# Sparse attention into a gated feed-forward layer: the softmax reciprocals of units 2 to 7 spread over the partitions by VectorE's shuffle instead of through DRAM, in a new order of all instructions

## The chip, the cores and the metric

One core of a Trainium2 chip runs the whole kernel in one launch. The metric is the device time of an execution in microseconds (us). Engines are TensorE (PE in the profile; PEld is its weight load), VectorE (DVE), ScalarE (ACT), GpSimd (POOL) and SyncE (SP). SP here only issues DMAs; four more are issued from ScalarE's queue at the start.

## The reference

Batch 4, 8 heads, 768 positions, head width 64. Heads 0, 2 and 6 ("retrieval") attend to all earlier positions, the other five only to the first 4 positions ("sinks") and to a window of 64. Then the heads are laid side by side and a two-matrix layer follows.

```python
scores = scale * np.matmul(q, k.transpose(0, 1, 3, 2))      # 4 x 8 x 768 x 768
stream_keep = causal & (is_sink | in_win)                     # sink: pos < 4, window: 0 <= rel < 64
mask = np.where(retrieval head, causal, stream_keep)
a = np.exp(scores - max); a = a / (sum(a) + 1e-9)             # where mask, else 0
x = np.matmul(a, v)  ->  (3072, 512)
h = x @ w_in                                                 # 512 x 2048
g = h * (1.0 / (1.0 + np.exp(-beta * h)))
out = g @ w_out                                              # 2048 x 512, float32
```

## The kernel before

**Units.** The work is cut into eight units: unit n is batch n // 2 and half u = n % 2 of the sequence, 384 positions. For each unit, `attention` loads q, k and v, casts them to bf16, brings q and k into head-width-major form (units 0 to 2 by TensorE transposes, units 3 to 7 by a transposing DMA, `turn_block`), computes scores transposed (`scores`, in "rounds" into one of two PSUM tiles `sp`), exponentials on ScalarE (`exps`, into tiles `es`), masks on VectorE (`masks`), sums over the keys by matmuls with selecting columns (`sums`, `sums_d`), and the product with v (`pv`). The result, normalized by the reciprocal of the sums, is `xT` (512 rows by 384 positions in bf16, four tiles of 128).

**The layer behind it.** `first` does one of 16 steps of the first product per unit: four matmuls of 128x384 (`mm1`), then `swish_a` (Tanh on ScalarE, tile `t`) and `swish_b` (VectorE, tile `gT`). A step needs a cast column block of w_in (`cast_w_in`, 16 pieces, four to a load) and all of `xT`. `second` does the product with w_out three matmuls at a time, `out_copy` and `out_store` end it.

**The reciprocals.** Units 0 and 1 (`recips`, `split`, `spread`, `norm_held`) spread the reciprocal over the partitions with matmuls. Units 2 to 7 did it like this: `sums_d` leaves eight rows of 384 sums in PSUM, `sums_copy` brings them to an SBUF tile `sc`, `sums_turn` turns them by DMA into a tile `rec` of 96x32, `recips_d` takes the reciprocal there, `spread_w` stores it to DRAM (`rd`), and `spread_r` reads it back so that each of the eight rows lies on 64 partitions of `R` (128 x 4 x 384 f32). On odd units one more part goes to a tile `RX`, since the last third of one head's product is computed on the other half of the partitions (`moved`). `norm` multiplies PSUM by `R` into `xT`. `R` is one buffer, so the next unit's spread waits for this unit's `norm`.

**The order.** Nothing is left to a scheduler. Every operation is added to a plan with what it needs, what it gives and which buffers it takes; `SEQUENCE` lists all operations in the order in which the plan takes them, and `CHOICE` says for some of them which of two or three engines runs them. The plan places each operation by costs written in `add`, and the instructions are issued in order of that placing. So each engine's queue is fixed in advance: an instruction that waits holds all that stand behind it on its engine. A matmul `fill` before some steps of units 0 and 1 repeats transposes of a constant for gaps that the plan foresees, and 25 such matmuls open the program. Rings say how many buffers a name has: `wf` (weights and later q, k, v blocks, 1 MB or 0.8 MB each) 3, `vf` 3, `q2f` and `k2f` 5, `b` (PSUM bank) 4, `sp` 2, `osb` 3, `R`, `rec` and `sc` 1.

All instructions are issued through one helper, so every line of the profile says L112, and groups are told apart by tile names.

Of the kernel before, what the change touches and what calls it, by code (L numbers as in the profile page):

```python
# [8 lines left out]
F32 = mybir.dt.float32  # L9
# [11 lines left out]
NQ = 384  # L21
# [7 lines left out]
QUARTERS = [[[1, 0], [2, 3], [4, 5], [6, 7]], [[2], [6], [0], [3, 5, 7, 1, 4]]]  # L29
ROWS = [16, 1]  # L30

NE = [16, 24]
ORDER = [[1, 0, 2, 3, 4, 5, 6, 7], [2, 6, 0, 3, 5, 7, 1, 4]]
# [4 lines left out]
    474, 475, 6, 466, 4, 8, 14, 468, 12, 478, 467, 20, 10, 0, 2, 16, 5, 469, 473, 9, 7, 33, 471, 29, 77, 34,  # L38
    31, 13, 89, 32, 15, 30, 37, 477, 18, 50, 38, 39, 51, 11, 79, 40, 85, 1, 56, 43, 52, 3, 490, 35, 25, 41,
    27, 36, 26, 57, 42, 28, 17, 44, 45, 21, 47, 78, 91, 48, 53, 80, 97, 54, 59, 86, 102, 480, 23, 100, 24,  # L40
    101, 58, 103, 60, 49, 116, 19, 46, 117, 118, 55, 61, 22, 120, 62, 463, 121, 485, 479, 492, 119, 122, 73,
    493, 90, 63, 92, 491, 123, 114, 75, 64, 74, 81, 115, 112, 76, 83, 125, 481, 65, 87, 126, 67, 113, 69, 484,
    66, 134, 482, 71, 68, 135, 483, 137, 108, 70, 500, 139, 109, 72, 488, 520, 82, 93, 524, 138, 84, 104, 464,
    140, 127, 489, 95, 465, 528, 521, 494, 105, 522, 529, 486, 532, 536, 495, 136, 525, 487, 530, 106, 142,
    526, 88, 533, 143, 534, 502, 540, 107, 98, 110, 503, 547, 505, 111, 94, 541, 128, 548, 131, 501, 542, 551,
    132, 124, 555, 141, 129, 96, 549, 556, 559, 133, 159, 130, 560, 504, 557, 99, 144, 552, 510, 499, 553,
    155, 145, 497, 537, 498, 538, 157, 156, 496, 146, 515, 507, 563, 158, 509, 561, 570, 508, 564, 160, 147,
    523, 571, 148, 506, 527, 565, 572, 163, 531, 167, 153, 149, 151, 511, 535, 171, 150, 512, 161, 152, 574,
    513, 165, 154, 578, 575, 514, 173, 582, 579, 576, 169, 580, 586, 583, 218, 518, 592, 584, 476, 587, 517,
    596, 588, 516, 470, 597, 519, 539, 593, 598, 162, 543, 546, 594, 168, 222, 550, 172, 554, 174, 170, 184,  # L50
    185, 558, 544, 164, 166, 562, 190, 186, 188, 191, 193, 175, 189, 566, 187, 600, 221, 196, 569, 573, 192,
    601, 577, 194, 581, 567, 219, 181, 602, 198, 220, 604, 199, 197, 182, 224, 608, 201, 200, 585, 609, 195,
    227, 225, 203, 605, 610, 589, 223, 204, 606, 228, 612, 202, 206, 590, 205, 619, 613, 207, 226, 176, 208,
    620, 177, 623, 621, 209, 591, 614, 210, 627, 631, 229, 628, 635, 632, 629, 237, 633, 636, 235, 642, 568,
    624, 637, 239, 646, 238, 650, 211, 647, 625, 240, 212, 178, 472, 269, 595, 651, 648, 241, 599, 652, 242,
    654, 179, 643, 249, 655, 603, 236, 252, 644, 213, 658, 250, 253, 607, 656, 659, 244, 660, 611, 247, 271,
    615, 245, 618, 622, 243, 251, 616, 254, 248, 273, 626, 180, 255, 630, 257, 183, 634, 246, 256, 638, 258,
    272, 641, 639, 259, 270, 617, 645, 260, 649, 261, 214, 216, 231, 215, 280, 653, 232, 657, 217, 275, 661,
    664, 662, 274, 278, 668, 665, 276, 672, 669, 666, 277, 676, 262, 673, 230, 233, 670, 674, 677, 279, 678,
    680, 684, 681, 691, 682, 263, 685, 695, 326, 692, 686, 699, 693, 696, 703, 700, 697, 707, 663, 701, 714,  # L60
    704, 708, 718, 289, 705, 709, 715, 722, 726, 716, 264, 723, 234, 667, 727, 290, 281, 671, 724, 293, 282,
    728, 675, 719, 283, 291, 730, 720, 679, 731, 292, 315, 284, 295, 732, 683, 296, 687, 298, 690, 694, 688,
    300, 297, 698, 319, 303, 294, 327, 301, 302, 702, 304, 328, 706, 265, 299, 329, 267, 266, 689, 305, 330,
    545, 268, 710, 306, 713, 717, 307, 721, 370, 725, 317, 736, 729, 737, 321, 740, 738, 316, 711, 733, 324,
    741, 744, 318, 734, 748, 320, 742, 745, 752, 322, 749, 746, 323, 756, 308, 753, 750, 763, 754, 325, 757,
    767, 764, 758, 771, 640, 765, 768, 775, 309, 772, 366, 769, 779, 773, 776, 786, 777, 790, 787, 286, 780,
    788, 334, 332, 285, 739, 335, 287, 794, 336, 781, 743, 795, 310, 337, 791, 796, 747, 338, 792, 798, 339,
    369, 802, 799, 346, 367, 803, 800, 751, 349, 373, 368, 804, 755, 347, 376, 759, 762, 288, 760, 341, 372,
    766, 344, 333, 375, 770, 340, 342, 371, 774, 343, 374, 351, 350, 345, 778, 354, 348, 377, 782, 352, 785,
    311, 353, 355, 313, 312, 356, 789, 357, 314, 793, 358, 386, 797, 331, 387, 735, 801, 390, 712, 412, 808,  # L70
    388, 812, 809, 378, 392, 813, 810, 805, 395, 379, 814, 816, 391, 783, 359, 380, 820, 806, 817, 360, 824,
    416, 821, 818, 828, 822, 825, 835, 393, 826, 839, 396, 829, 836, 397, 830, 843, 389, 837, 840, 847, 361,
    844, 841, 851, 394, 848, 845, 415, 858, 849, 862, 852, 413, 859, 866, 853, 414, 860, 870, 863, 417, 864,
    400, 811, 419, 871, 815, 398, 418, 872, 422, 819, 867, 823, 868, 421, 399, 874, 401, 381, 827, 875, 420,
    402, 876, 362, 403, 404, 364, 363, 761, 831, 834, 423, 365, 838, 842, 429, 846, 880, 832, 850, 405, 881,
    431, 406, 882, 884, 807, 432, 382, 383, 888, 885, 892, 889, 886, 384, 854, 424, 890, 893, 857, 433, 861,
    426, 833, 855, 865, 407, 894, 869, 385, 896, 900, 425, 897, 434, 898, 907, 436, 911, 901, 784, 908, 873,
    902, 856, 877, 909, 912, 915, 878, 913, 919, 430, 916, 879, 427, 923, 920, 917, 930, 924, 921, 934, 435,
    925, 938, 931, 942, 932, 939, 408, 943, 940, 410, 409, 935, 883, 887, 411, 946, 944, 443, 936, 947, 891,
    895, 446, 447, 948, 952, 444, 953, 438, 954, 899, 441, 903, 439, 956, 442, 445, 906, 957, 448, 437, 958,  # L80
    910, 449, 914, 451, 450, 440, 918, 904, 960, 452, 453, 922, 454, 961, 926, 455, 964, 962, 968, 965, 905,
    929, 969, 933, 966, 937, 970, 428, 941, 945, 927, 949, 456, 972, 928, 950, 457, 979, 973, 983, 980, 974,
    987, 981, 984, 991, 988, 985, 995, 989, 992, 1002, 996, 993, 458, 1006, 997, 1003, 1010, 1007, 1004, 1014,
    1008, 1018, 1015, 955, 1011, 1016, 1012, 1019, 951, 1020, 959, 963, 967, 971, 975, 978, 976, 982, 977,
    986, 990, 994, 998, 1001, 999, 1005, 459, 460, 1000, 461, 1009, 462, 1013, 1017, 1021, 1024, 1022, 1028,
    1025, 1023, 1032, 1029, 1026, 1036, 1030, 1033, 1040, 1037, 1034, 1044, 1038, 1041, 1051, 1045, 1042,
    1055, 1046, 1052, 1059, 1056, 1053, 1063, 1057, 1060, 1067, 1064, 1061, 1073, 1065, 1068, 1076, 1069,
    1079, 1077, 1027, 1080, 1078, 1031, 1081, 1074, 1082, 1075, 1085, 1083, 1035, 1086, 1084, 1039, 1087,
    1043, 1047, 1048, 1050, 1054, 1049, 1058, 1062, 1066, 1070, 1088, 1071, 1089, 1072, 1092, 1090, 1091,
    1093, 1094, 1095,  # L90
]
CHOICE = (
    "aaddagaggdgdadadadaadddaddaaddgaagggdaaadaadaaaddaaaddaggdgdgaggadggdgdaadaadaaadaadadadddadddaaa"
# [95 lines left out]
def kernel(  # L189
# [68 lines left out]
    hl = consts.tile([96, NQ], BF16, name="hl")  # L258
# [49 lines left out]
    def const_zero():  # L308
        dve.memset(hl, 0.0)
        dve.memset(KP[2][:, 0:32 * (NP - 1)], 0.0)  # L310
# [185 lines left out]
    def load_beta():  # L496
        held["beta"] = rp.tile([128, NQ], F32, name="sc")[0:FO, 0:128]
        sp.dma_start(out=held["beta"], in_=moe_beta.rearrange("(fo fi) -> fo fi", fi=128))
# [278 lines left out]
    CR = NQ // 32  # L777

    def sums_turn(x):

        x.rec = rp.tile([8 * CR, 32], F32, name="rec")
        for p, step, c, n in ([(0, 16, 0, 8)], [(96, 1, 3, 5), (0, 32, 0, 3)])[x.u]:
            sp.dma_start(out=x.rec[c * CR:(c + n) * CR, :],
                         in_=x.sc[p:p + (n - 1) * step + 1:step, :].rearrange("p (c n) -> p c n", n=32))
# [4 lines left out]
    def spread_w(x):  # L789
        x.rd = dp.tile([8, NQ], F32, name="rd")  # L790
        sp.dma_start(out=x.rd.rearrange("h (c n) -> (h c) n", n=32), in_=x.rec)

    def spread_r(x):
        x.R = rp.tile([128, NP, NQ], F32, name="R", bufs=RINGS["R"])
        src = x.rd[:]
        at = [[ORDER[x.u].index(XT[t][i]) for t in range(NP)] for i in range(2)]
# [444 lines left out]
```

## Time and profile before

| | |
|---|---|
| median of 3 runs | 240.53 us (240.43 to 241.18) |
| span of the profiled execution | 238.9 us |
| its own time | not listed beside the span; the median is 1.6 us above the span |
| TensorE | 224.3 us busy (94%), mean granted clock 0.979 |
| VectorE | 153.9 us (64%) |
| ScalarE | 141.9 us (59%) |
| GpSimd | 90.8 us (38%) |
| DMA | 43.14 MB moved, 92108 packets, 75936 of them under 512 B |

A group's line has the engine, the operation, tile out <- tiles in, the shapes and the count; then the busy time in us and the mean ns of one; then the idle time of the engine just before, and what ended it. A timeline line has the start, the time from the first to the last of a merged group, the engine and operation. A window line has the stretch, its length, then each engine's busy time with its instructions, TensorE's granted clock (1.00 is full), the mean busy share of the 16 DMA engines and GB/s.

### The profile page before, as it was taken

How to read it: one execution, taken by the hardware profiler on the slowest of the kernel's cores; microseconds unless marked ns; L12 is line 12 of the kernel's file. 1: busy time of each engine (PE TensorE's matmuls, PEld its weight loads, DVE VectorE, ACT ScalarE, POOL GpSimd, SP SyncE). 2: the span in 40 equal slices, each digit the busy share in tenths (PEclk: the TensorE clock that was granted, in tenths of full speed). 3: DMA queues.
4: the chain of work that ended last, by engine and by line, in shares of the span. 5: the costliest groups of instructions: out<-in, count | busy, mean ns of one | idle time of the engine just before them, and what ended most of it. 6: DMA issues, size and time to landing. Idle time of an engine off the chain costs nothing.

```text
span 238.9 us, 6057 instructions
## 1 busy us (share of the span) xinstructions
PE 224.3 (94%) x2359; PEld 128.6 (54%) x2385; DVE 153.9 (64%) x354; ACT 141.9 (59%) x238; POOL 90.8 (38%) x199
## 2 busy tenths in 40 slices
PE   8678996999999999999999999999999999999994
PEld 8535555555555456546544545564465555466553
DVE  4539869783968838865686548787475477157620
ACT  3858785456889518761679569707677437107611
POOL 7204759587632845696536173403600000000000
PEclk9956999999999999999999999999999999999999
DMA  6999699999989979999998999789910026211012
GB/s 197 273 307 321 205 258 354 300 314 211 175 196 240 211 162 189 214 230 223 225 231 179 169 230 231 149 178 216 219 71 3 0 92 150 80 44 47 0 44 88
DMA packets 92108, 43.14 MB, mean 181 GB/s; under 512 B 75936, under 2 KB 84848, under 8 KB 92080
## 3 DMA queue, kind: packets, MB, share of 16 engines
q1 hardware_dynamic: 90992, 41.98, 76.0%
q10 hardware_dynamic: 1088, 0.79, 1.1%
q8 instruction: 18, 0.29, 0.5%
q14 instruction: 10, 0.08, 0.1%
HBM read 32.38 MB, written 6.37 MB: 162 GB/s over the span
## 4 chain that ended last, share of the span: by engine, by line
PE 70%; DMA 9%; DVE 8%; SPq 4%; POOL 3%; ACT 3%; issue 2%; POOLq 0%
PE b L112 60%; PE sp L112 10%; SPq L112 4%; DMA QK<-c 3%; DMA wf<-in_v_dram 2%; POOL c L112 2%; DMA wf<-in_k_dram 2%; DMA q2f<-in_q_dram 2%; DVE es L112 2%; DVE gT L112 1%; ACT t L112 1%; DVE vs L112 1%; DVE QK L112 1%; ACT es L112 1%; DVE KP L112 1%
## 5 line engine op out<-in xcount | busy, mean ns | idle before, releaser
L112 ACT ACTIVATE t<-b,beta_h 128x384 f32<-128x384 f32 x128 | 72.4, 582 | 40.3 <-PE b L112 29.2
L112 DVE SCALAR_TENSOR_TENSOR gT<-t,b 128x384 bf16<-128x384 f32 x128 | 68.9, 551 | 37.1 <-ACT t L112 33.2
L112 PE MATMUL b<-xT,w_in 128*128 128x384 bf16 x512 | 90.3, 326 | 1.4 <-POOL w_in L112 0.9
L112 PE MATMUL b<-w_out,gT 128*128 128x512 bf16 (+1 forms) x374 | 87.1, 370 | 2.7 <-issue 1.8
L112 PEld LDWEIGHTS <-w_in 128*128 128x128 bf16 x512 | 49.0, 98 | 38.7 <-issue 2.6
L112 PEld LDWEIGHTS <-gT 128*128 128x128 bf16 x400 | 36.9, 98 | 38.7 <-issue 2.4
L112 ACT ACTIVATE es<-sp 128x768 bf16<-128x768 f32 (+3 forms) x64 | 49.1, 806 | 11.1 <-PE sp L112 10.7
L112 POOL CAST c<-wf 128x256 bf16<-128x256 f32 x60 | 23.2, 432 | 21.2 <-DMA wf<-in_q_dram 13.7
L112 PE MATMUL sp<-QK 64*64 64x64 bf16 (+6 forms) x402 | 19.9, 242 | 4.0 <-DVE QK L112 1.5
L112 ACT ACTIVATE osb<-b 128x512 f32<-128x512 f32 (+1 forms) x14 | 8.0, 568 | 23.9 <-PE b L112 16.9
L112 PEld LDWEIGHTS <-QK 64*64 64x64 bf16 (+1 forms) x402 | 10.4, 107 | 15.2 <-issue 12.1
L112 POOL COPY KP<-QK 128x64 bf16<-128x64 bf16 (+4 forms) x36 | 10.2, 332 | 21.6 <-DMA QK<-c 21.6
L112 POOL CAST w_in<-wf 128x512 bf16<-128x512 f32 x16 | 10.7, 699 | 15.2 <-DMA wf<-in_moe_w_in_dram 15.2
L112 POOL CAST vb<-wf 128x512 bf16<-128x512 f32 x18 | 12.2, 696 | 11.2 <-DMA wf<-in_v_dram 11.1
L112 DVE TENSOR_TENSOR es<-es,mask_c 128x256 bf16<-128x256 bf16 (+2 forms) x32 | 12.1, 394 | 4.2 <-ACT es L112 4.0
L112 DVE TENSOR_TENSOR es<-es,mask_s 128x800 bf16<-128x800 bf16 (+5 forms) x24 | 12.9, 551 | 2.7 <-ACT es L112 2.7
L112 DVE TENSOR_TENSOR xT<-sp,R 128x768 bf16<-128x768 f32 (+3 forms) x18 | 11.6, 687 | 4.0 <-PE sp L112 3.9
L112 DVE TENSOR_SCALAR osb<-b 128x512 f32<-128x512 f32 x11 | 7.5, 681 | 9.9 <-PE b L112 7.7
L112 PE MATMUL sp<-es,vb 128*64 128x64 bf16 (+3 forms) x243 | 13.8, 237 | 0.0
L112 POOL COPY vs<-vb 64x1536 bf16<-64x1536 bf16 (+2 forms) x9 | 12.2, 1361 | 2.5 <-issue 2.1
L112 PEld LDWEIGHTS <-vb 128*64 128x64 bf16 x243 | 11.8, 111 | 0.3
L112 POOL CAST w_out<-wf 128x512 bf16<-128x512 f32 x16 | 10.1, 667 | 2.2 <-DMA wf<-in_moe_w_out_dram 2.1
(91 smaller groups left out, 169.8 us busy)
## 6 DMA issues: line engine op xcount, KB each, us to landing
out_dram<-osb SPq DMA_DIRECT2D x23, 256.0 KB
wf<-in_v_dram SPq DMA_DIRECT2D x18, 256.0 KB
wf<-in_moe_w_out_dram SPq DMA_DIRECT2D x4, 1024.0 KB
wf<-in_q_dram SPq DMA_DIRECT2D x15, 256.0 KB
wf<-in_k_dram SPq DMA_DIRECT2D x15, 256.0 KB
R<-rd SPq DMA_DIRECT2D x9, 384.0 KB
wf<-in_moe_w_in_dram SPq DMA_DIRECT2D x4, 768.0 KB
q2f<-in_q_dram SPq DMA_DIRECT2D x12, 192.0 KB
```

Of the source, the lines that this page charges most:

```text
L112: ins = f(*a, **k)
```

## The change

`spread_w` and `spread_r` go. In their place `spread_rows` issues four DMAs that bring the reciprocals from `rec` into four rows of `R` (partitions 0, 32, 64, 96), and `spread_lanes` runs VectorE's `stream_shuffle` in place, once for each half of `R`, with a mask that gives every lane of a group of 32 the group's first lane; on odd units a third, small one serves `RX`, which now lies ahead of `R` in the same tile. The order of rows in `rec` (`QUARTERS`, `TURNS`) and the order of the four parts in `R` are changed to fit. `R` is now allocated once; the tile `hl` of units 0 and 1 is put into `sc`'s buffer, and beta is loaded by way of a `t` tile. Four planned DMA costs are altered (in `dma=`), and `SEQUENCE` and `CHOICE` are replaced whole, for units 0 and 1 and for the layer too.

```diff
-QUARTERS = [[[1, 0], [2, 3], [4, 5], [6, 7]], [[2], [6], [0], [3, 5, 7, 1, 4]]]
+QUARTERS = [[[1, 0], [4, 5], [2, 3], [6, 7]], [[2], [6], [0], [5, 1, 4, 3, 7]]]
+TURNS = [[(0, 32, 0, 4), (16, 32, 4, 4)], [(97, 1, 0, 2), (0, 32, 2, 4), (99, 1, 6, 2)]]
...
-        for p, step, c, n in ([(0, 16, 0, 8)], [(96, 1, 3, 5), (0, 32, 0, 3)])[x.u]:
+        for p, step, c, n in TURNS[x.u]:
             sp.dma_start(out=x.rec[c * CR:(c + n) * CR, :],
                          in_=x.sc[p:p + (n - 1) * step + 1:step, :].rearrange("p (c n) -> p c n", n=32))
...
-    def spread_w(x):
-        x.rd = dp.tile([8, NQ], F32, name="rd")
-        sp.dma_start(out=x.rd.rearrange("h (c n) -> (h c) n", n=32), in_=x.rec)
-    def spread_r(x):
-        x.R = rp.tile([128, NP, NQ], F32, name="R", bufs=RINGS["R"])
...
-                sp.dma_start(out=x.R[i * D:(i + 1) * D, t, :],
-                             in_=bass.AP(src.tensor, src.offset + a[0] * NQ, [[0, D], [(a[1] - a[0]) * NQ, len(a)], [1, NQ]]))
...
+    def spread_rows(x):
+        f = new_R()
+        x.R, x.RX = f[:, XC:].rearrange("p (k n) -> p k n", k=NP), f[:, 0:XC]
         for i in range(2):
...
+            c0 = (0 if i == 0 else NP * CR) - (XC // 32 if i and x.u else 0)
+            c1 = (i + 1) * NP * CR
+            for r in (i * D, i * D + 32):
+                sp.dma_start(out=f[r:r + 1, XC + NP * NQ - (c1 - c0) * 32:].rearrange("p (c n) -> p c n", n=32),
+                             in_=x.rec[c0:c1, :])
+    def spread_lanes(x, g):
+        def lanes(v):
+            dve.stream_shuffle(out=v, in_=v, mask=[0] * 32)
+        lanes(x.R[:, g::2, :])
+        if g and x.u:
+            lanes(x.RX[D:128, :])
...
-            add("sp", 0.4, lambda: spread_w(x), needs=[("rec", n)], gives=[("rd", n)], dma=0.1, drop=[("rec", n)])
-            add("sp", [1.33, 2.65][u], lambda: spread_r(x), needs=[("rd", n)], gives=[("R", n, t) for t in range(NP)], dma=[6.2, 6.0][u],
-                take=[("R", n, 2)] + ([("q2f", (n, "x"), 1)] if u else []))
+            add("sp", 1.7, lambda: spread_rows(x), needs=[("rec", n)], gives=[("rd", n)], dma=0.1,
+                take=[("R", n, 2)], drop=[("rec", n)])
+            for g in range(2):
+                add("dve", 1.25 if u and g else 0.95, lambda g=g: spread_lanes(x, g), needs=[("rd", n)] + ([("R", n, 0)] if g else []),
+                    gives=[("R", n, 2 * g), ("R", n, 2 * g + 1)])
```

In the new order all scores of unit 1 stand ahead of the first step of the first product on TensorE's queue (before, the steps began among them), and SP's queue has all q and k of units 0 and 1 ahead of the first block of w_in, with three of the four w_in blocks ahead of v of unit 1, the fourth behind it and the w_out blocks after that (before, w_in and w_out blocks alternated among the loads of unit 1).

## The prediction

> **What bounds the kernel now.** I read the page first: busy shares, then the 40 slices.
>
> ```profile
> span 238.9 us, 6057 instructions
> PE 224.3 (94%) x2359; PEld 128.6 (54%) x2385; DVE 153.9 (64%) x354; ACT 141.9 (59%) x238; POOL 90.8 (38%) x199
> ...
> PE   8678996999999999999999999999999999999994
> ...
> PEclk9956999999999999999999999999999999999999
> DMA  6999699999989979999998999789910026211012
> ```
>
> TensorE is the bound: from the eighth slice (42 us) to the last but one it is at nine tenths or more. What is lost lies ahead of that and in the last 3 us. The windows by stage price it.
>
> ```profile
> 0.00:10.00 10.00, 7.71 (x99) 6.99 (x99) 4.25 (x27) 5.50 (x11) 4.71 (x28) 1.00 0.89 227
> 10.00:20.00 10.00, 6.85 (x63) 3.64 (x63) 5.85 (x18) 6.58 (x11) 1.61 (x3) 0.61 1.13 307
> 20.00:30.00 10.00, 9.35 (x140) 6.19 (x139) 9.20 (x20) 8.18 (x13) 6.96 (x11) 0.88 0.80 249
> 30.00:43.00 13.00, 10.92 (x186) 7.13 (x185) 10.90 (x21) 8.95 (x16) 9.07 (x16) 1.00 1.07 312
> ...
> 90.00:130.00 40.00, 38.86 (x394) 21.45 (x397) 27.94 (x55) 26.95 (x47) 24.14 (x50) 1.00 1.05 212
> 130.00:170.00 40.00, 39.41 (x450) 21.67 (x453) 27.62 (x67) 23.28 (x39) 15.64 (x36) 1.00 0.99 195
> ```
>
> The second column is TensorE's busy time, the last three the granted clock, DMA share and GB/s. TensorE idles 8.2 us before 43, partly at clock 0.61, but only 1.7 us in 90 to 170, with the DMA engines full there. So relief for DMA or for another engine past 43 us is worth at most those gaps; the price of this change is decided by (1) how early the new order fills TensorE and (2) what new wait it puts into the steady part. The timeline has the terms:
>
> ```profile
> 19.57 2.50 POOL L112 CAST w_in<-wf 128x512 bf16<-128x512 f32 x3 [7.73 <-DMA wf<-in_moe_w_in_dram]
> 25.01 2.29 POOL L112 CAST w_in<-wf 128x512 bf16<-128x512 f32 x4 [2.94 <-DMA wf<-in_moe_w_in_dram]
> 27.98 1.47 PE L112 MATMUL b<-xT,w_in 128*128 128x384 bf16 x8
> 39.08 1.51 DVE L112 COPY vs<-vb 64x1536 bf16<-64x1536 bf16 x2
> 43.12 1.48 PE L112 MATMUL b<-xT,w_in 128*128 128x384 bf16 x8
> 47.69 4.19 PE L112 MATMUL b<-xT,w_in 128*128 128x384 bf16 x24
> ```
>
> The first w_in block lands at 19.57, the second at 25.01, the first product step (`first`, four matmuls) starts at 27.98, and at 43.12 TensorE has done all attention of units 0 and 1 but four spread matmuls, and ten steps. A step costs 4.19/6 = 0.70 us.
>
> **The spread itself, part by part.** Removed, for each of units 2 to 7: `spread_w` (1 DMA) and `spread_r` (2 or 4 DMAs), 0.4 and 1.3 to 2.6 us of SP's queue, and 4.8 MB of 43.1 MB in all. Added: one more DMA in `sums_turn`, four small DMAs (48 or 52 runs of 128 B each, to one row per quadrant), and on VectorE two shuffles of 128x768 f32, on odd units a third of 64x128: twelve and three. No shuffle is in the trace. Nearest rows:
>
> ```profile
> L112 DVE TENSOR_TENSOR xT<-sp,R 128x768 bf16<-128x768 f32 x9 | 8.3, 954 | 4.0 <-PE sp L112 3.9
> L112 DVE TENSOR_TENSOR es<-es,mask_s 128x768 bf16<-128x768 bf16 x4 | 2.5, 652 | 0.0
> L112 DVE COPY R<-sp 128x768 f32<-128x768 f32 x1 | 1.0, 957 | 0.0
> ```
>
> Bounds 0.65 and, were a second pass needed, 1.9 us; I take 0.95 (same size, type and one element a step) and 0.3 for the small ones (the 64x128 rows are 0.29): 12 x 0.95 + 3 x 0.3 = 12.3 us more for VectorE, from 8 to 23 us. It has 64% busy time and hides this while TensorE is the bound; the whole is lost only if VectorE were full, and it waits 33.2 us on ScalarE's `t` tiles. Of the DMA relief I take nothing: the cover is TensorE's backlog of products; its most is the 1.7 us above.
>
> The Trainium skill, "VectorE: DVE Perf Modes" (The perf-mode tier table), gives the shuffle only the single-rate program, about 2400 ns at 2048 elements. By an estimate from that page's 0.96 GHz, 768 elements take 1.07 us, which would make VectorE's addition 14 us and leave my time as it is.
>
> **The head.** Here I follow the order of every queue in the changed program. SP now issues all q and k of units 0 and 1, three v tiles and one q tile of unit 2 before the first w_in block: 17 x 0.197 + 3 x 0.262 + 1.05 = 5.18 MB until it has landed. Before, 4.19 MB had been asked for when a block landed at 19.57, and 5.70 MB when the next did at 25.01: 0.278 MB/us. The slices from 36 to 54 us show 0.30 to 0.35. So the blocks land at 23.1, 26.9, 30.7; v of unit 1 at 34.2; the fourth block at 38.0 (at 0.278), or at 22.8, 26.1, 29.5, 32.6 and 36 (at 0.31).
>
> ScalarE needs up to the last exponential of unit 1: 9 copies or casts at 0.5, 16 exponentials at 0.81 and one at 0.5, 2 holds at 0.8: 19.6 us from its first cast at 5.1, so 25 us or later. VectorE: the last v tile of unit 0 lands about 18.6 (3.93 MB), then cast 0.42, `vs` 1.92, `hl` 1.34, mask and copy 0.84, four `xT` 2.2: 25.2. First step then about 25.5, against 27.98. TensorE goes on with steps 0 to 11 as w_in is cast (0.62 a tile), up to 34.5; unit 1's PV waits for v 34.2, cast 0.62, `vs` 1.51: 36.3 plus 2.45 gives 38.8; spreads, unit 2's first scores and steps 12 to 14 end near 42 (41.4 at the faster rate). At 42 it has 15 steps, the spreads (0.8), and 0.75 us of unit 2. Before would get there at 43.1 + 5 x 0.70 + 0.8 + 0.75 = 48.2. Gain 6.2. Next stand 13 steps of unit 1, 9.1 us, with ScalarE nearly full; the second product first needs the third w_out block on the queue, landing near 50.0 and cast by 52.9, while TensorE arrives at 51.2: 1.7 lost at the slow rate, nothing at the fast (w_out cast by 49.7). Head gain 6.2 - 1.7 = 4.5 to 48.2 - 41.4 = 6.8; I take 5, nearer the slow rate, which is the one measured in this stretch.
>
> The row of clock 0.61 in 10 to 20 us shows that gaps here lower the granted clock, and the new order has 33 fewer filler matmuls. "TensorE: Matmul & The Clock Gate" (Part 1: The HAM clock gate) says about 3.4 us idle halves the clock, and that as long a busy stretch restores it. By that rule a cold start of the steps would cost an estimated 1.7 us, making my time 238.2.
>
> **The new wait.** VectorE's shuffle waits in its queue for the four small DMAs; masks and `gT` stand behind it, TensorE behind those. SP issues them behind whatever load stands there.
>
> ```profile
> 72.81 0.38 SPq L112 DMA_DIRECT2D rd<-rec  x1
> 73.24 2.47 SPq L112 DMA_DIRECT2D wf<-in_q_dram  x3
> 76.26 1.34 SPq L112 DMA_DIRECT2D R<-rd  x2
> 77.70 6.83 SPq L112 DMA_DIRECT2D wf<-in_k_dram  x3
> ```
>
> A small DMA lands in 1.4 (unit 7: issued until 196.0, seen at 197.4) to 3.3 us. A load of three holds SP 2.5 to 6.8 us. Unit 2, from the end of its sums: copy 0.7, turn 1.5, then SP has a q load, two stores and an edge load (4.8 to 9.1), four issues 2.0, landing 1.4 to 3.3, shuffles and masks 2.5, `xT` 1.9: 14.8 to 21.0. TensorE's own work until it needs `xT` is, by the order, 42 product matmuls at 0.22 (87.1 us over 400), five score rounds (2.3), PV 1.2 and sums 0.9: 13.6. So 1.2 to 7.4 us of stall; I take 1.5, nearest the quiet rows, as the former 0.8 MB spread no longer fills the queue. Units 3 to 7 have 16 to 20 us of other matmuls between and a chain of 11 to 19: 0 to 0.9 for unit 3, 0 to 0.8 for unit 4, else nothing. I take 0.5 of gain from the spare 1.7 us for the other reshuffling.
>
> **Sum.** 238.9 - 5 + 1.5 - 0.5 = 234.9 us of span. The page gives only the span of its execution; the median of the runs is 240.53, 1.6 above. So 236.5.
>
> **Rivals.**
> - The shuffle's wait wins: a load holds SP 6.8 us before unit 2's rows and landing takes 3.3 us. Stalls 7.4 + 0.9 + 0.8 = 9.1, against a head gain of 5: 244.6. It decides once the stalls pass 5 us. For: the 6.83 row. Against: that load queued behind an R transfer that is gone. Chance 0.18.
> - The head is not bound by loads but by ScalarE and VectorE, which need 19.6 and some 20 us of the 20.5 available; idle before 25 us (before, ScalarE was busy 12.1 of 20) moves the first step to 28.5 and takes 3 us: 239.5, or 240.5 and over with 1 us more of stall. Chance 0.15, split to both sides.
> - No stall at unit 2 and the faster load rate: 238.9 - 6.8 - 1.7 + 1.6 = 232.0. Chance 0.17.
> - The change not doing what it says: the changed program holds the fifteen shuffles and no transfer to DRAM for R, so nothing is left for this.
>
> **Numbers.** Forecast 0.5. About 0.3% (0.7 us) is what a measurement tells from no change. Faster: 0.5 + 0.17 + 0.04 = 0.71; same 0.06; slower 0.18 + 0.05 = 0.23. Range 232.0 to 242.0: from the third rival to a stall of 7 us at unit 2, leaving most of the first rival out.
>
> **What would show it.** Right: first step near 25.5 us; TensorE busy without gaps of over 2 us from 35 to 55; a pause of TensorE on VectorE's `xT` for unit 2, between 70 and 82 us, and hardly one later; shuffles at 0.95 us; q1's bytes down by a tenth. Wrong: w_in casts later than 24 us, TensorE waiting on w_out past 53, or VectorE waiting several us on the R rows for each unit.

## The result and the profile after

The changed kernel is slower: 243.92 us (median of 4 runs, 243.02 to 244.44) against 240.86 us (4 runs, 240.43 to 241.50) for the kernel before on the same chip. The ratio is 1.0141, with a 95% interval from 1.0101 to 1.0182. I had forecast 236.5 us and a gain; the time lies outside my range, on the other side. A ratio leaves out runs more than 1.5% above the fastest of the same kernel and a median does not, so the two can differ, most in e12_late_load_no_spread (0.7%).

The page of the changed kernel, the lines that answer to those shown of before:

```profile
span 242.0 us, 6040 instructions
PE 221.8 (92%) x2327; PEld 125.8 (52%) x2352; DVE 161.5 (67%) x390; ACT 138.9 (57%) x232; POOL 87.8 (36%) x200
...
PE   7788888899999888797999899999999999999995
...
PEclk9979999999999999999999999999999999999999
DMA  6999999999999396889979971746901011031022
```

The nines of TensorE's row now start at the ninth slice, but there are weak slices between the 14th and the 23rd (79 to 139 us), where before there were only nines. The DMA row has holes in the same stretch. The windows by stage give it in us; the second column is TensorE's busy time, the last three are TensorE's granted clock, the DMA share and GB/s.

```profile
10.00:20.00 10.00, 8.45 (x115) 5.04 (x115) 7.96 (x22) 7.62 (x13) 4.35 (x9) 0.83 1.03 255
30.00:43.00 13.00, 11.01 (x163) 6.65 (x161) 8.93 (x19) 7.12 (x12) 6.72 (x12) 1.00 0.98 271
90.00:130.00 40.00, 35.32 (x416) 19.55 (x418) 30.78 (x76) 27.79 (x47) 18.44 (x40) 1.00 0.91 171
130.00:170.00 40.00, 38.64 (x404) 21.61 (x409) 28.90 (x61) 21.95 (x38) 15.27 (x32) 1.00 0.66 135
```

TensorE idles 4.7 us in 90 to 130, where it idled 1.1 before. The head came as forecast; the timeline's w_in casts and first product steps:

```profile
23.58 2.29 POOL L112 CAST w_in<-wf 128x512 bf16<-128x512 f32 x4 [5.15 <-DMA wf<-in_moe_w_in_dram]
27.43 2.29 POOL L112 CAST w_in<-wf 128x512 bf16<-128x512 f32 x4 [1.55 <-DMA wf<-in_moe_w_in_dram]
...
25.71 5.63 PE L112 MATMUL b<-xT,w_in 128*128 128x384 bf16 x32
```

**Where the time went.** I measure a lead: by how much earlier the product with v (PV) of unit n ends on TensorE, plus the product matmuls that the new order has put ahead of that point, minus those that it has put behind it, at 0.16 us (w_in) and 0.22 us (w_out) each. The two prices are the marginal ones of the trace: 4 matmuls take 0.82 us and 8 take 1.47; 3 take 0.82 and 9 take 2.12. The numbers of matmuls come from the order of instructions (7 more w_in ahead of unit 1's PV, 34 fewer w_out and 3 fewer w_in ahead of unit 7's).

| lead in us at the end of PV of unit | 1 | 2 | 3 | 4 | 5 | 7 |
|---|---|---|---|---|---|---|
| changed kernel | 4.6 | 3.1 | -0.9 | -1.8 | -3.2 | -3.3 |

The last one agrees with the spans (242.0 against 238.9). So the head gain was there, 1.5 of it went up to unit 2, and 6.4 us were lost behind it, nearly all up to unit 5. What TensorE waited for there, from the table of waits (us in total, times, longest), and the worst case of it:

```profile
PE sp L112 <- DMA QK<-c: 5.3, 3, 2.4
...
98.16 0.50 PE L112 MATMUL sp<-QK 64*128 64x384 bf16 x6 [2.41 <-DMA QK<-c]
```

These are the first scores of units 4, 5 and 6, waiting for the transposing DMA of their own q and k; before, this wait was 0.5 us in all. The transposes come late for TensorE because of the queue that issues them. SyncE's timeline (start, time over the group, transfers in it):

```profile
71.33 1.31 SPq L112 DMA_DIRECT2D rec<-sc  x2
72.69 1.71 SPq L112 DMA_DIRECT2D wf<-in_q_dram  x3
...
77.78 2.51 SPq L112 DMA_DIRECT2D R<-rec  x4
80.34 1.18 SPq L112 DMA_DIRECT2D vf<-in_v_dram  x3
81.61 2.72 SPq L112 DMA_DIRECT2D wf<-in_k_dram  x3
...
85.24 2.76 SPq L112 DMA_DIRECT2D wf<-in_q_dram  x3
88.04 1.73 SPq L112 DMA_DIRECT2D vf<-in_v_dram  x3
89.88 1.29 SPq L112 DMA_TRANSPOSE QK<-c  x1
```

There is hardly a gap from 71 us on (issues fill 56.6 of the 60 us from 70 to 130). Unit 2's rows stand for 2.5 us ahead of unit 4's k (81.61), and unit 5's q and an edge load (`vf`, small parts of v) for 4.5 us ahead of unit 4's transposes (89.88). The kernel before sent these three transposes at the same time:

```profile
89.59 6.12 SPq L112 DMA_TRANSPOSE QK<-c  x3
```

Its queue was as full (55.8 of the same 60 us). So TensorE came to unit 4 some 3 us earlier, and unit 4's inputs did not. In the chain that ended last SyncE's own issuing has 13% of the span, against 4% before, and TensorE 54% against 70%.

What I had feared instead did not happen. The shuffles took what I had put down, and VectorE waited for their rows 0.9 us in all; a group's line, and what ended the idle time ahead of instructions on `R`:

```profile
L112 DVE STREAM_SHUFFLE R<-R 128x768 f32<-128x768 f32 x12 | 11.8, 1017 | 0.0
...
  DMA R<-rec: 0.9, 2
```

### The profile page after: what moved, and what is told of

Same layout as the page of the kernel before. It is cut to its first block, busy times and chain, and to the rows that moved or that the text cites. A ratio compares the mean times of both kernels' runs of the same rounds, so it can differ in the third digit from the quotient of the medians.

```text
span 242.0 us, 6040 instructions
## 1 busy us (share of the span) xinstructions
PE 221.8 (92%) x2327; PEld 125.8 (52%) x2352; DVE 161.5 (67%) x390; ACT 138.9 (57%) x232; POOL 87.8 (36%) x200
## 3 DMA queue, kind: packets, MB, share of 16 engines
q1 hardware_dynamic: 88886, 37.24, 66.4%
## 4 chain that ended last, share of the span: by engine, by line
PE 54%; DMA 21%; SPq 13%; POOL 4%; DVE 4%; issue 3%; ACT 1%; POOLq 0%; DVEq 0%
PE b L112 49%; SPq L112 13%; DMA wf<-in_moe_w_in_dram 10%; PE sp L112 4%; DMA QK<-c 4%; DMA wf<-in_k_dram 3%; DMA q2f<-in_q_dram 2%; POOL c L112 2%; DMA wf<-in_v_dram 2%; DVE es L112 1%; DVE QK L112 1%; POOL w_in L112 1%; DVE c L112 1%; DVE mask_s L112 1%; POOL vs L112 1%
## 5 line engine op out<-in xcount | busy, mean ns | idle before, releaser
L112 PE MATMUL b<-xT,w_in 128*128 128x384 bf16 x512 | 91.5, 326 | 3.5 <-POOL w_in L112 2.0
L112 POOL CAST c<-wf 128x256 bf16<-128x256 f32 x60 | 24.9, 463 | 22.9 <-DMA wf<-in_k_dram 18.6
L112 PE MATMUL sp<-QK 64*64 64x64 bf16 (+7 forms) x402 | 19.5, 237 | 6.7 <-DMA QK<-c 5.3
L112 ACT ACTIVATE osb<-b 128x512 f32<-128x512 f32 (+1 forms) x18 | 10.6, 589 | 25.9 <-PE b L112 25.9
L112 DVE TENSOR_TENSOR es<-es,mask_c 128x256 bf16<-128x256 bf16 (+2 forms) x32 | 9.9, 331 | 10.0 <-ACT es L112 10.0
L112 DVE TENSOR_TENSOR xT<-sp,R 128x768 bf16<-128x768 f32 (+3 forms) x21 | 12.7, 630 | 3.5 <-PE sp L112 3.3
L112 POOL CAST w_in<-wf 128x512 bf16<-128x512 f32 x16 | 9.2, 625 | 12.6 <-DMA wf<-in_moe_w_in_dram 12.6
L112 DVE TENSOR_SCALAR osb<-b 128x512 f32<-128x512 f32 (+1 forms) x7 | 4.6, 653 | 12.4 <-PE b L112 10.1
L112 DVE STREAM_SHUFFLE R<-R 128x768 f32<-128x768 f32 (+1 forms) x15 | 12.7, 873 | 0.1
L112 POOL COPY KP<-QK 128x64 bf16<-128x64 bf16 (+5 forms) x32 | 8.4, 305 | 9.1 <-DMA QK<-c 8.4
```

Of the source, the lines that this page charges most:

```text
L112: ins = f(*a, **k)
```

## The experiments

The theories were "queue" (the row transfers on SyncE), "order" (where the new order puts loads and scores) and "VectorE" (the shuffles). Ratios are to the kernel before, with the 95% interval; a per cent is 2.4 us.

**Spread and order apart.**

`e1_old_order`: the new spread with the SEQUENCE and CHOICE of before.

> The spread by shuffle, but the instructions in the order of the kernel before (the four row transfers stand where the write to DRAM stood, the shuffles where the DRAM reads of R were first needed). It separates the new spread from the new order. Theory 'queue' (the row transfers and their place between the loads on SyncE's queue cost the time): the loss stays although the head is the old one, 243.5 us or more. Theory 'order' (the new order has loads and scores of units 3 to 6 standing so that TensorE waits on their transposes): the loss goes, 239.5 to 241.0 us. Theory 'VectorE' (2 us of shuffles per unit hold masks and gT back): 242 to 245 us, with TensorE waiting on DVE tiles xT and es.

Measured: 244.61 us, 1.0149 (1.0114 to 1.0185). "Order" falls as the only cause: with the old order the loss is the same. But here it has another form. TensorE's waits name VectorE:

```profile
PE b L112 <- DVE gT L112: 3.8, 6, 1.4
```

From 90.2 to 106.4 us VectorE has no gap: behind a full stretch of `gT` stand the shuffles at 100.34 and 103.05, 1.0 us each, among `gT` and masks.

`e2_no_spread`:

```diff
-                sp.dma_start(out=f[r:r + 1, ...], in_=x.rec[c0:c1, :])
...
-            dve.stream_shuffle(out=v, in_=v, mask=[0] * 32)
```

> The changed kernel with units 2 to 7 not spread at all: no row transfers and no shuffles, so R keeps what the last spread of unit 1 left and the output is normalised by the wrong reciprocals. Everything else, the order too, as in the changed kernel. Theory 'queue': SyncE's queue loses 24 issues of 0.6 us, the next units' loads come earlier, and the time falls to 237 to 240 us. Theory 'order': TensorE still waits on the transposes of units 4 to 6, 242.5 to 244 us. Theory 'VectorE': VectorE loses 12.7 us of shuffles, 238 to 241 us, with the waits on SyncE's transposes left as they are.

Measured: 240.17 us, 0.9936 (0.9901 to 0.9971), so the whole spread costs 4.9 us in the new order (1.0141 - 0.9936 of 240.9; 3.7 by the medians), and the new order without any spread is worth only 1.5 us. The wait for the transposes falls from 5.3 to 1.8 us. The queue shows the price directly: from unit 2's sums to unit 6's transposes SyncE issues the same 55 transfers in the same order, over 49.2 us here (1.1 of it a wait at the end) and over 55.4 us in the changed kernel, where twelve rows stand among them and hold it for 9.0.

These prices are against no spread at all. The path through DRAM held the queue too: it had as many transfers as the rows, 24, and their issues took 14.6 us in the kernel before, where the rows take 16.8. The turn of the sums, with six transfers more, went from 7.2 to 9.7 us. So the change put some 4.8 us on SyncE's queue, not 16.8.

`e3_rows_on_act`: `act.dma_start` for the rows.

> The changed kernel with the four row transfers of each spread issued by ScalarE instead of SyncE, at the same place in the order. Theory 'queue': SyncE's loads no longer stand behind the 24 issues, 239.5 to 242 us. Theory 'order': no gain, 243.5 us or more, since ScalarE now spends the issue time and waits for the sums' turn in its own queue. Theory 'VectorE': 243.5 to 244.5 us.

Measured: 265.07 us, 1.0995 (1.0948 to 1.1041). ScalarE spends 3.3 and 6.4 us on the rows of units 2 and 3, which SyncE issued in 2.5 and 3.9, with exponentials queued behind them; TensorE waits 10.5 us for exponentials, and VectorE 12.9 us for rows. No expectation came near it; only "order" (243.5 or more) had left room for it.

`e4_scores_later`: three operations moved in SEQUENCE.

> The changed kernel with the first score round of units 4, 5 and 6 moved back on TensorE, behind 8 to 14 product matmuls that stand ready (unit 4 behind the second product's seventh group, unit 5 behind step 4 of the third first product, unit 6 behind the first of the fourth); all else as in the changed kernel. Theory 'order': the 5.3 us that TensorE waits on the transposes of q and k of these units are filled, 239.5 to 242 us. Theory 'queue': the inputs are still late and the wait shows later in the unit; 242.5 to 244 us. Theory 'VectorE': 243 to 244.5 us.

Measured: 246.11 us, 1.0210 (1.0172 to 1.0248), worse than the changed kernel. The wait for transposes is gone from TensorE's table, and 5.2 us of waits for exponentials stand in its place: the scores came later, so all behind them did. "Order" in the form "a filler in the gap would do" is refuted.

**The two halves of the spread.**

`e5_rows_only`: the shuffle's line out. `e6_shuffles_only`: the rows' lines out.

> The changed kernel without its fifteen shuffles; the 24 row transfers and the order stay, so R is right in four of its rows only and the output is not normalised. With e2_no_spread (neither rows nor shuffles, 240.2 us against 243.9) it divides the 3.7 us between the two. Theory 'queue' (SyncE's issues and their place between the loads): nothing is gained, 243 to 244 us, and TensorE still waits for the transposes of units 4 to 6. Theory 'VectorE' (12.7 us of shuffles delay masks and gT, and what waits on them): all of it is gained, 240 to 241 us.

> The changed kernel without the 24 row transfers; the fifteen shuffles and the order stay (R holds old values, so the reciprocals are wrong). Theory 'queue': 240 to 241 us. Theory 'VectorE': 243 to 244 us. If both parts only cost together (the shuffle waits behind late rows), it and e5_rows_only both give 240 to 241 us.

Measured: rows alone 244.44 us, 1.0130 (1.0086 to 1.0174); shuffles alone 241.66 us, 0.9997 (0.9965 to 1.0030). In the new order the loss is mostly the rows': they add 4.7 us to e2_no_spread and 3.5 to the kernel with shuffles. The shuffles alone cost 1.5 us, and nothing that can be measured on top of the rows. "Queue" holds. Where the rows are out, `xT` no longer waits for them to land either, but in the changed kernel VectorE waited only 0.9 us for that.

`e8_old_order_rows`: e1_old_order without the shuffle's line.

> As e1_old_order (new spread, order of the kernel before), but without the fifteen shuffles; the rows are sent, R is right in four rows only. Theory 'VectorE': in e1_old_order TensorE waited 3.8 us on VectorE's gT in six places (1.1 us in two before), so the shuffles are the loss, and 240.5 to 241 us are left, or less, since 4.8 MB are not moved. Theory 'queue': 243.5 to 244.6 us.

Measured: 242.29 us, 1.0026 (0.9994 to 1.0058). In the old order it is the other way round: rows in place of the path through DRAM cost 0.6 us (interval from nothing to 1.4), and the shuffles put 3.0 us on top. "VectorE" holds there. So which engine pays for the same edit depends on the order around it.

`e7_order_only`: the kernel before with the new SEQUENCE and CHOICE; I put the reads of `R` one item behind the write.

> The spread of the kernel before (through DRAM, 128 lanes read back) with the new order and the new choice of engines; the reads of R stand one SyncE item behind the write of the reciprocals, for unit 7 directly behind it. It is the other half of e1_old_order. If spread and order add up, as e1_old_order (new spread, old order, 244.6) suggests, the order alone gives 240 us, 0.7 less than the kernel before. If the new order pays only with the shuffle, because the DRAM spread's 4.8 MB collide with its loads, 242 to 246 us. If the order has the head gain that I predicted, 236 to 238 us.

Measured: 254.78 us, 1.0591 (1.0539 to 1.0643). SyncE waits 7.2 us for the stored reciprocals and then spends 6.5 us on issuing unit 4's k; TensorE waits 8.2 us on `xT`. The places of the reads were mine, so this shows neither what the path through DRAM costs in the new order with better places, nor what another order could do. Its lead was 5.3 us at unit 1 and 5.2 at unit 2, and -5.9 at unit 3.

The lead of the profiled executions side by side:

| lead at PV of unit | 1 | 2 | 3 | 5 | 7 |
|---|---|---|---|---|---|
| changed kernel | 4.6 | 3.1 | -0.9 | -3.2 | -3.3 |
| e2: no rows, no shuffles | 3.7 | 3.1 | -0.2 | 0.5 | 0.5 |
| e6: shuffles | 3.5 | 4.5 | -0.3 | 0.0 | -1.1 |
| e5: rows | 3.2 | 0.1 | -3.0 | -5.2 | -5.2 |
| e1: old order, both | -0.2 | -0.1 | -1.7 | -2.6 | -3.2 |
| e8: old order, rows | 0.5 | 0.3 | 0.3 | 1.3 | -0.5 |

Every kernel of this table with the new order loses 3 to 5 us between unit 2 and unit 3, with or without a spread. With rows it loses 2 more up to unit 5.

**What about a row transfer costs.**

`e10_fewer_issues`: on units 2, 4 and 6 one transfer fills two rows.

```diff
-            for r in (i * D, i * D + 32):
+            for r in (i * D, i * D + 32) if x.u else (32 * i,):
+                p, c0, c1 = (slice(r, r + 1), c0, c1) if x.u else (slice(r, r + D + 1, D), 0, 2 * NP * CR)
```

> The changed kernel with the four row transfers of units 2, 4 and 6 sent as two, each to two rows: 18 issues instead of 24, the same bytes and runs of 128 B. Theory 'SyncE's issue time' (0.6 us each, 3.7 to 4.2 us lost to 24 of them): about a quarter comes back, 242.7 to 243.3 us. Theory 'the wait for the reciprocals in SyncE's order' (loads stand behind a wait, whatever is issued after it): 243.7 to 244.3 us.

`e11_tiny_rows`: `in_=x.rec[c0:c0 + 1, :]` to 32 columns.

> The changed kernel with 24 row transfers of one run of 128 B each instead of 48 or 52 (so most of R is not filled and the output is not normalised). Issues and waits stay, the runs go. Theory 'the wait in SyncE's order': 243.5 to 244.3 us. Theory 'the runs' (1,200 runs of 128 B on the DMA engines, and SyncE's time grows with them): 241 to 242 us, near e6_shuffles_only (241.7).

Measured: e10 244.25 us, 1.0116 (1.0068 to 1.0165), which can't be told from the changed kernel or from a gain of a quarter; inconclusive. e11 243.96 us, 1.0122 (1.0069 to 1.0174): with one run in place of 48 nothing came back. So the runs of a row are not the price. The issues say the same, e11 first, then the changed kernel (min/median/max in ns):

```profile
L112 SPq DMA_DIRECT2D R<-rec x24: 527/587/1564, 78.1 to 199.5; - x24
```
```profile
L112 SPq DMA_DIRECT2D R<-rec x24: 530/592/1469, 77.8 to 199.8; - x24
```

A row costs the queue 0.59 us at the median, with 48 runs or with one.

`e15_double_issues`: each row in two halves.

```diff
+                h = (c0 + c1) // 2
+                for a, z in ((c0, h), (h, c1)):
+                    o = XC + NP * NQ - (c1 - a) * 32
+                    sp.dma_start(out=f[r:r + 1, o:o + (z - a) * 32]..., in_=x.rec[a:z, :])
```

> The changed kernel with each of the 24 row transfers cut in two, so 48 issues with the same bytes, runs and waits. Theory 'SyncE's issue time': the 24 issues cost 3.7 to 4.2 us, so 24 more cost 3 to 5 us, 247 to 249 us. Theory 'the wait for the reciprocals in SyncE's order': 243.5 to 244.5 us.

Measured: 258.46 us, 1.0683 (1.0640 to 1.0726). Far more than "issue time" had: 13 us over the changed kernel. The wait for the reciprocals is the same (SyncE waits 3.8 us for `rec`, 3.5 in the changed kernel), so it does not explain this; and in the changed kernel those waits stand at 147 and 198 us, behind the loss, while from 71.4 to 134 us no two issues of SyncE are more than 0.11 us apart. The eight issues of unit 2 in its SyncE timeline, 2.51 us for four before:

```profile
77.94 6.38 SPq L112 DMA_DIRECT2D R<-rec  x8
```

The 48 take 0.74 us each at the median and 36.3 us in all, where the 24 took 16.8: 19.4 us more of queue for 13 us more of time. The first 24 cost 4.9 us for 16.8, so there was some slack in the queue, and less was left behind them. VectorE waits 15.5 us for rows in this run, so the shuffle's wait that I had feared is there. But from 78 to 114 us the chain that ended last does not go through it: it goes through the rows' issues to what stands behind them, unit 2's last edge load (for `VE`) and then an output store that frees ScalarE's `osb` ahead of an exponential.

```profile
PE sp L112 <- POOL VE L112: 5.5, 1, 5.5
```

In the changed kernel this wait was 0.9 us.

**Other issues on the full queue.**

`e9_late_load`: two loads and one cast moved in SEQUENCE. `e12_late_load_no_spread`: the same in e2_no_spread.

> The changed kernel with two loads moved back on SyncE's queue: q of unit 5 and the edge load that follows it stand behind the three transposes of unit 4 instead of ahead of them (and the one cast on GpSimd that waits for that q behind unit 3's copy). Every kernel with the new order, with or without rows and shuffles, loses 3.1 to 4.7 us of lead between the PV of unit 2 and that of unit 3. Theory 'supply' (unit 4's q and k stand behind unit 5's load on SyncE, which holds the queue 2.8 to 4.9 us): unit 4's scores come 2 to 4 us earlier, 241 to 242 us. Theory 'the rows alone': no change, 243.5 to 244.5 us.

> e2_no_spread (240.2 us) with the two loads moved back as in e9_late_load; units 2 to 7 are not spread, so R is not filled. Theory 'supply': the lead of 3.1 us at unit 2 is kept past unit 3, 237 to 238.5 us, which is what the new head is worth where nothing else is late. Theory that the lead is lost elsewhere: 239.5 to 241 us.

Measured: e9 244.04 us, 1.0112 (1.0076 to 1.0149). The transposes were issued at 86.5 and 90.1 us (89.9 and 93.5 in the changed kernel), as intended, but TensorE then waited for an exponential, ScalarE for the buffer of an output copy, and that for a store which now stood behind the moved loads:

```profile
107.28 0.60 ACT L112 ACTIVATE osb<-b 128x512 f32<-128x512 f32 x1 [5.25 <-DMA out_dram<-osb]
```

e9's time is that of "the rows alone". e12: 239.04 us, 0.9861 (0.9797 to 0.9925), 1.8 us below e2 by the ratios though the intervals meet. So it points to "supply", that where no rows stand in the queue some of the gain is kept, but does not show it.

`e13_stores_on_act`: 13 stores issued by ScalarE; `e14_stores_late_load`: that with e9's moves.

```diff
+                st = "act" if (n, ns) in ACT_STORES else "sp"
-                add("sp", 0.4, lambda ns=ns: out_store(x, ns), needs=[("ob", n, ns)], dma=0.7,
+                add(st, 0.4, lambda ns=ns, st=st: out_store(x, ns, ENG[st]), needs=[("ob", n, ns)], dma=0.7,
```

> The changed kernel with 13 output stores of units 0 to 4 (those whose copy ScalarE makes) issued by ScalarE right behind its copy, instead of standing in SyncE's queue; rows, shuffles and the rest of the order stay. Theory 'SyncE's queue is full' (from 71 to 136 us it issues almost without a gap, so each issue ahead of a load puts TensorE's next unit off): 13 issues of 0.5 to 0.7 us fewer, 240.5 to 242.5 us. Theory 'the wait for the reciprocals': no change, 243 to 244.5 us. Against both: ScalarE pays the issues itself, up to 245 us.

> e13_stores_on_act with the two loads of e9_late_load moved back too. In e9_late_load the transposes came 3.3 us earlier, but TensorE then waited 3.8 us on ScalarE, which waited for a store that stood behind the moved loads; with the stores off that queue the gain should stay. Theory 'SyncE's queue is full': 239 to 241.5 us, below e13_stores_on_act. Otherwise 243 to 245 us.

Measured: 256.80 us, 1.0615 (1.0579 to 1.0651), and 254.51 us, 1.0547 (1.0506 to 1.0587). Both my theories missed. ScalarE paid only 0.34 us an issue. But SyncE's queue now waited for the landing of stores that another engine had issued:

```profile
SPq L115 <- DMA out_dram<-osb: 15.5, 6, 5.3
```

The trace shows why: the 192 transfers of the program signal eight semaphores in turn, 24 on each, ScalarE's among them, and 97 of SyncE's 175 in this run wait for the semaphore that they will signal themselves, so for the transfer eight places earlier, whichever of the two engines issued it. A small transfer takes one of the eight places as a load of 256 KB does. From 70 to 134 us seven issues of SyncE were held by this, for 14.1 us. In the changed kernel none of the 74 issues of this stretch was: the transfer eight places earlier had always landed. So there a row costs the queue its issue, and not its place among the eight.

`e16_store_first`, `e17_store_fewer`, `e18_load_before_sums`: one store ahead of the moved load; then also e10's rows; then also unit 4's q ahead of unit 2's sums.

> e9_late_load with one store (unit 1, tile 0) moved ahead of the load of unit 5's q, so that ScalarE does not wait for its buffer. Theory 'SyncE's issue time': what e9_late_load gained at the transposes is kept now, 1 to 3 us below the changed kernel: 241 to 243 us. If each move on the full queue only names the next wait, 243 to 244.5 us.

> e16_store_first with the 18 row issues of e10_fewer_issues. Theory 'SyncE's issue time': three times two issues of 0.59 us fewer, of which two times two lie before 136 us: 1 to 2.4 us below e16_store_first.

> e17_store_fewer with the load of unit 4's q ahead of the transfer of unit 2's sums on SyncE. In the changed kernel SyncE stands idle from 69.4 to 71.3 us waiting for those sums, and the load behind it takes 1.7 us. Theory 'SyncE's issue time': all that follows on the queue comes up to 1.7 us earlier, 0.5 to 1.7 us below e17_store_fewer. If the load holds the queue when the sums are ready, unit 2's rows are late, and it is 0 to 2 us slower.

Measured: 243.36 us, 1.0086 (1.0049 to 1.0124); 243.30 us, 1.0106 (1.0059 to 1.0153); 242.70 us, 1.0070 (1.0039 to 1.0101). Single steps are within the intervals (e17 had been expected 1 to 2.4 us below e16, and was not); the three together take half of the loss away, 1.7 us (1.2 by the medians), by moving four items on SyncE's queue and sending six rows fewer. The lead at unit 3 is 2.3 to 2.9 us in the three, where the changed kernel had -0.9. None of the runs beats the kernel before except e2 and e12, which have no spread.

## Why the prediction was wrong, step by step

**The head: right in its times, its size partly by luck.** First step forecast for 25.5 us, found at 25.71; casts of w_in for 23.1 and 26.9, found at 23.58 and 27.43; PV of unit 1 for 38.8, found at 39.69. Taken gain 5, lead 4.6 at unit 1; in the other profiles with the new order it is 2.3 to 5.3. But the 5 was 6.2 up to 42 us less 1.7 for a wait on w_out. The lead did not reach 6.2 (TensorE waited 1.1 us at 41.2 for the fourth w_in block), and no wait on w_out came: the second product began at 53.4 us without one. The cold start of the steps did not come either: the clock was 1.00 from 20 to 30 us, and the first 32 matmuls took 5.63 us, 0.70 a step.

**Unit 2's wait: right in size, by luck.** I took 1.5 us; the lead fell by 1.5. The way to it was not mine: SyncE sent the rows at 77.8, VectorE waited 0.5 us for them, and TensorE did not wait on `xT` there but 0.9 us on `VE`, whose edge load stood behind the rows. Without shuffles (e5) the lead fell by 3.1.

**The shuffle's price: right; its cover: half right.** I took 0.95 us and found 1.02. The estimate of 1.07 us from the Trainium skill, "VectorE: DVE Perf Modes" (The perf-mode tier table), was about as near; its single rate for shuffles agrees with the 1.02 us. "VectorE hides this while TensorE is the bound" is true in the new order with rows (e5 and the changed kernel can't be told apart) and false in the old (3.0 us).

**DMA relief taken as nothing: right.** q1's bytes fell from 41.98 to 37.24 MB and the DMA share in 90 to 130 from full to 0.91, and no gain in time shows it.

**The failed step: "Units 3 to 7 ... else nothing. I take 0.5 of gain."** With it the sum carried the head's 5 us to the end, whole but for unit 2's 1.5. In its place 6.4 us were lost behind unit 2. I had priced SyncE's issues only in the chain of `R` ("four issues 2.0") and asked who waits for the rows. I did not ask who stands behind them: the k of unit 4, its transposes, and with them TensorE two units on. The lines were in the profile of before: the same timeline that I showed has SyncE issuing from 72.81 to 84.5 with 0.7 us of gaps, and 37 of the 40 us from 90 to 130 are filled in that profile too. I read that queue as the place of a delay and not as a resource that was used up.

Two things are missing from the sum. The first is that a lead at unit 2 is no gain by itself: TensorE had by then done 93 of the 96 w_out matmuls of units 0 and 1, so what it had left was unit 2's own product and units 3 and 4, whose loads stand in a queue that no part of the change made faster (unit 4's transposes at 89.9 us, 89.6 before, 88.9 with no spread at all). That took 3.3 us between unit 2 and 3 in e2 and 4.0 in the changed kernel, and it leaves 1.5 us of the head's gain even without a spread. The second is the queue's price for the rows: 4.9 us for the whole spread in the new order. I had taken the DRAM transfers off and put the rows on without setting their issues against each other: 14.6 us went and 16.8 came, with 2.5 more for the turn of the sums. What the DRAM path costs in the new order no run shows; in the old order the rows cost 0.6 us more than it. The two terms overlap, so they do not add up to what the runs give for each; with -4.6 for the head, 1.5 up to unit 2 and 6.4 for both, the sum is 238.9 + 3.3 = 242.2, against 242.0 found. Why the lead goes even in e2 is less sure than that it goes: its DMA share from 90 to 130 us is 1.09, so there the DMA engines may set the pace of the queue.

**The rivals.** "The shuffle's wait wins" has nearly the measured time (244.6) for the wrong reason: its stalls of 9.1 us on `R` were 0.9. "Head bound by ScalarE and VectorE" did not come, nor did the faster load rate: the first two w_in blocks came 0.5 us behind even the slow one. The change did what it says.

**The solid track.** SyncE's track was solid in this case's profile before and after, and the doubled issues show what that can cost: 19.4 us more of issuing, 13 us more of time. The Trainium skill, "Perfetto Trace Analysis" (What "DMA-bound" means), lists the issuing sequencer as a bound of its own, to be known by a track that is solid with DMA slices. A solid track alone was not yet a bound here: before, TensorE lost only 1.1 us from 90 to 130. The page adds that large descriptors are what matter then; here 48 runs and one run cost 592 and 587 ns, so for the rows the number of transfers mattered and not their make-up. It also says that balancing over the issuing engines may help (DMA Optimizations); it did not in either form that I ran: 265.1 us for the rows, 256.8 for the stores.

## What to carry to other kernels

When an edit puts transfers on a queue, ask not only when they land but how much of that queue's time is free in the same stretch, and who stands behind them; a queue without gaps has no room for a head start of the others, even if the page's busy shares do not list it. Fewer bytes bought nothing here: 4.7 MB less, but as many transfers for the spread and six more for the sums. Set the issues that go against those that come. And a gain at the head has to be followed to the end: when TensorE has used up the work that is ready, the lead goes into the next wait.

## What was not expected of the hardware

The granted clock between 10 and 20 us differs from execution to execution of the same head: 0.83 in the changed kernel, 1.00 in e5 and e11, 0.65 in e9, with PV of unit 0 ending at 22.9, 21.1, 21.1 and 25.0. So a single profile's head is known to about 2 us either way, and a time's run-to-run width (239.5 to 244.7 for the kernel before over all comparisons) is as large as what I wanted to forecast. "TensorE: Matmul & The Clock Gate" (Part 1: The HAM clock gate) ties the clock to stretches of idleness; that fits some of the gaps here, but no run isolates it, and my reading of the 0.61 does not hold by itself: the old head ran at 0.61 before and at 1.00 in e8, with TensorE busy for 6.9 and 6.1 of the 10 us.

A shuffle's preparatory instruction takes 13 ns at the median, next to nothing beside the shuffle's 1.02 us. An issue of a transfer within SBUF took 0.59 us, of an output store on ScalarE's queue 0.34 (e13).
